# First layer's weights converted with an accumulating DMA, and one output chunk by seven products

## The chip, the cores and the metric

The kernel runs on 1 core of one Trainium2 chip. The metric is the device time of one execution in microseconds (us), the median of 3 runs. TensorE does the matrix products, VectorE (DVE) and ScalarE (ACT) the elementwise work, GpSimd (POOL) and SyncE (SP) issue transfers.

## The reference, cut to what matters

An attention over channels, then two feed-forward layers on 6016 tokens of 256 channels, all float32:

```
qn = q / (norm(q, axis=1) + 1e-6);  kn = k / (norm(k, axis=1) + 1e-6)
a  = softmax(kn^T @ qn / tau)            # 256 x 256
x  = (v @ a) as 6016 x 256
x  = gelu_sigmoid(x @ w_in) @ w_out      # layer 0: 256 -> 2048 -> 256
h  = x @ w2_in
out = (max(h, 0) + alpha * min(h, 0)) @ w2_out   # layer 1, same shapes
```

The weights are given as float64 and reach the kernel as pairs of 32-bit words.

## The kernel before

**Numbers in two parts.** Every operand of a product is a pair (hi, lo) of the fast 32-bit matmul type; a product is three matmuls, hi by hi, hi by lo and lo by hi (`PASSES`).

**Tiling.** The tokens are cut in 12 chunks, taken in 6 pairs, and each layer runs pair by pair. For each pair the hidden width is cut in 8 chunks j = 0 to 7 (`NQ`). For one j the kernel makes four hidden blocks ("units") and adds their share of the output (`Outs`, 8 steps of three matmuls; those of j run between the products of j + 1). The first pair of layer 0 goes by `direct`: each unit is two products, eight per j. All other pairs go by `quartet`: seven products per j (Strassen's scheme), on sums and differences of the operands, which `prepare` (tokens) and `combine_wi` (weights) build. In `quartet` the first product's result is copied from one PSUM bank to another by ScalarE, so that two later products add to it (`nc.scalar.copy(b, a)`, the copy of line 827, called "the fork copy" below).

**A unit in `direct`.** ScalarE takes the product out of PSUM (`act`, L761, writes `g`), rounds it to `ghi` (`high`, L775); VectorE writes the rest `glo` (`low`, L781), which the output step of the next j reads. Between `high` and `low`, `beside` puts background work for about 2.1 us on VectorE. ScalarE work that this asks for is kept in `put_off` and issued in one go at the start of the next `beside`, so after the next unit's `high`. Engines run in the order in which the program was written; a waiting instruction holds all behind it on its engine. Unit (j, u) below is the u-th of chunk j.

**Converting a weight piece.** During the first pair the background work is the conversion of layer 0's weights. A piece (class `Convert`) is 128 x 512 numbers of two words each: inner pieces ia0 to ia7 are one j's columns of `w_in`, outer pieces ob0 to ob7 one j's rows of `w_out`; from the fifth on, two neighbours are done as one piece of 1024. SP loads the raw words (2 `raw` buffers); ScalarE makes `p` from the high word (L130); VectorE does six steps: `shift` (L133), `signed` (L137, writes `top`), `power` (L147), `rest` (L150, puts the low word's share in `p`), `less` (L166), `low` (L169, writes the lo part). Between `signed` and `less` ScalarE rounds `top` to the hi part (`copy`, L143). A load goes out when the `rest` of the piece that had its buffer is done.

**What waits for a piece.** `emit_w(j)` (j up to 3) and `emit_pair(4)`, `emit_pair(6)` multiply ia pieces by the softmax's transpose on TensorE (L483, L628), and ScalarE (`keep_hi`, L491) and VectorE (`keep_lo`, L495) bring the result to `WI`, the inner weights that the units use. They stand after unit (j - 1, 1). The outer pieces feed the output steps of their j directly (`WO`).

Of the kernel before, what the change touches and what calls it, by code (L numbers as in the profile page):

```python
# [34 lines left out]
TAIL = 12  # L35
ON_VECTOR = (4, 5, 6, 8)
# [20 lines left out]
def attention_then_two_ffns(ctx: ExitStack, tc: tile.TileContext, q, k, vT, tau, w1i, w1o, w2i, w2o, alpha, outT):  # L57
# [45 lines left out]
    class Convert:  # L103
# [4 lines left out]
        most = 2 * PIECE  # L108
        pool = None

        def __init__(self, src, pair, done=None):
            self.src, self.pair, self.done = src, pair, done
            self.made = False
            self.a = src.shape[1]
            self.n = self.a * src.shape[2]
# [7 lines left out]
        def load(self):  # L123
            self.raw = self.tile("raw", U32, RAWS, 2)
            nc.sync.dma_start(self.raw.rearrange("p (a n) w -> p a (n w)", a=self.a), u32(self.src))

        def scale(self):

            self.p = self.tile("p", F32, 2)
# [5 lines left out]
        def signed(self):  # L135
            self.top = self.tile("top", F32, 1)
            nc.vector.scalar_tensor_tensor(u32(self.top), self.raw[:, :, 1], 0x80000000, u32(self.p),  # L137
                                           ALU.bitwise_and, ALU.bitwise_or)
            self.hi, self.lo = self.pair()
            put_off.append(self.copy)  # L140

        def copy(self):
            nc.scalar.copy(self.hi, self.like(self.top))  # L143
# [30 lines left out]
    class Converter:  # L174


        STEPS = (("shift", 0.45), ("signed", 0.7), ("power", 0.45), ("rest", 0.7), ("less", 0.7), ("low", 0.7))

        def __init__(self):
            self.todo, self.loaded, self.ready, self.open, self.at = [], [], [], None, 0  # L180

# [3 lines left out]
        def load(self):  # L185

            while self.todo and len(self.loaded) + len(self.ready) + self.held < RAWS:
# [4 lines left out]
        def scale(self):  # L192
            if self.loaded and not self.ready:
# [3 lines left out]

        def cost(self):
            return self.time(self.open or (self.ready + self.loaded + self.todo)[0])

        def time(self, piece):
            t = self.STEPS[self.at][1]
            return 2 * t - 0.15 if piece.n > PIECE else t

        def waits(self):

            if not self.open:
# [5 lines left out]
        def needs(self):  # L213
            return [self.ready[0].scale] if self.at == 0 else [self.open.copy] if self.at == 4 else []

        def step(self):

            if self.waits():
                scalar_work()
            if not self.open:  # L220
                self.open = self.ready.pop(0)
                self.held = 1
            do, t = self.STEPS[self.at][0], self.time(self.open)
            getattr(self.open, do)()
            self.at += 1
            if do == "rest":
                self.held = 0
                self.scale()
                if self.ahead:
                    self.load()  # L230
            if self.at == len(self.STEPS):
# [11 lines left out]
        def left(self):  # L243
            return self.todo + self.loaded + self.ready + [x for x in (self.open,) if x]
# [10 lines left out]
    with tc.manual_schedule():  # L255
# [15 lines left out]
        def inner(j, n=1):  # L271
# [8 lines left out]
            return Convert(w1i.rearrange("p (a n) -> p a n", a=2)[:, :, j * C:(j + n) * C], pair)  # L280

        def outer(j, n=1):
            def pair():
                return tuple(WO[:, j:j + n, h].rearrange("p q a b -> p q (a b)") if n > 1 else flat(WO[:, j, h]) for h in range(2))
            return Convert(w1o[:, j * PIECE:(j + n) * PIECE].rearrange("p (a n) -> p a n", a=1), pair)

        ia, ob_ = {}, {}
        for made, piece, spans in ((ia, inner, ((0, 1), (1, 1), (2, 1), (3, 1), (4, 2), (6, 2))),
                                   (ob_, outer, ((0, 1), (1, 1), (2, 1), (3, 1), (4, 2), (6, 2)))):
# [3 lines left out]
        conv.todo = [ia[1], ob_[0], ia[2], ob_[1], ia[3], ob_[2], ia[4], ob_[3], ob_[4], ia[6], ob_[6]]  # L293
# [19 lines left out]
        def operand(pool=None):  # L313
# [3 lines left out]
            slot[0] += 1  # L317
            return xin[i > 3].tile([P, 2, T], F32R, tag=f"x{i}", name="x")
# [225 lines left out]
        def prepare(l, p):  # L544
# [4 lines left out]
            ops = operands[l, p] = {}  # L549
# [40 lines left out]
            ]  # L590
            return early, late
# [191 lines left out]
        def direct(j, outs, mid_way):  # L783

            ops = operands[0, 0]
            units = []
            for i, (f, c) in enumerate((f, c) for f in range(2) for c in range(2)):
# [12 lines left out]
                beside(FIRST, convert=True)  # L800
# [4 lines left out]
        def quartet(l, p, j, outs, carry):  # L805
# [3 lines left out]
            late = steps_late if j == 0 else []  # L809

# [3 lines left out]
            def copy(ps):  # L814
                s = sp.tile([P, T], F32, tag="s", name="s", bufs=3)
# [285 lines left out]
```

## Time and profile before

| | |
|---|---|
| median of 3 runs | 1034.37 us (1034.36 to 1034.7) |
| the profiled execution | 1034.38 us |
| its span, first to last instruction | 1032.6 us |
| TensorE matmul busy | 1027.4 us |
| VectorE busy | 765.3 us |
| ScalarE busy | 752.8 us |
| GpSimd busy | 31.3 us |
| granted TensorE clock | 1.000 over the span |

How to read it: 1.8 us of the execution lie outside the span. The matmuls of the first pair begin at about 50 us and those of the second pair at about 142 us, all times from the span's start. A matmul row in the timeline gives the time at which it began and how long it took; the next one begins before it ends, so whether TensorE lost time is read from the distances between beginnings. An idle time in square brackets names what ended it.

### The profile page before, as it was taken

Reading aid. Unit: us, or ns where it says so; the run is one execution under the profiler, and the core shown is the slowest. Engines: PE = TensorE matmul, PEld = TensorE weight load, DVE = VectorE, ACT = ScalarE, POOL = GpSimd, SP = SyncE. Lnnn points to the kernel's source line nnn. Section 1 sums busy time; section 2 is a strip of 40 time slices with the busy share of each in tenths; the row PEclk is TensorE's granted clock in tenths of the full one; section 3 lists DMA queues with packets and bytes.
Section 4 is the critical chain, followed back from the end, with each engine's and each line's share of the span. In section 5 each row is a group of like instructions: output and inputs, shape, how many; then the busy total and the mean of one; then the engine's idle time right before and its main releaser. Section 6 shows DMA issues by size and latency. Waiting matters only on the chain.

```text
span 1032.6 us, 12486 instructions
## 1 busy us (share of the span) xinstructions
PE 1027.4 (99%) x4640; PEld 866.8 (84%) x4640; DVE 765.3 (74%) x1230; ACT 752.8 (73%) x1255; POOL 31.3 (3%) x42
## 2 busy tenths in 40 slices
PE   9999999999999999999999999999999999999998
PEld 8888888888888888888998888888888888888997
DVE  4889967878778787445637777787877787877766
ACT  6777767778777777666767777777777777867776
POOL 4400000000000000000100000000000000000000
PEclk9999999999999999999999999999999999999999
DMA  9635102125224323003543001001001000000101
GB/s 361 240 106 180 42 23 95 42 77 179 77 82 158 101 93 133 1 1 126 200 169 113 1 21 62 1 21 62 1 21 62 1 18 25 35 0 1 42 1 36
DMA packets 30461, 77.62 MB, mean 75 GB/s; under 512 B 3008, under 2 KB 7616, under 8 KB 30144
## 3 DMA queue, kind: packets, MB, share of 16 engines
q1 hardware_dynamic: 28096, 65.29, 18.2%
q0 software_dynamic: 2304, 11.54, 3.4%
q8 instruction: 36, 0.59, 0.2%
q14 instruction: 25, 0.20, 0.1%
HBM read 52.96 MB, written 23.86 MB: 74 GB/s over the span
## 4 chain that ended last, share of the span: by engine, by line
PE 99%; DMA 0%; SPq 0%; ACT 0%; issue 0%
PE ps_o L713 50%; PE ps_h L684 44%; PE gram L348 4%; PE pw L483 1%; PE pw L628 1%; DMA qk<-in_k 0%; SPq L368 0%; PE nrm L426 0%; ACT s L730 0%; PE bc L448 0%; PE pt L471 0%
## 5 line engine op out<-in xcount | busy, mean ns | idle before, releaser
L713 PE MATMUL ps_o<-ghi,wo 128*128 128x512 f32 (+1 forms) x1536 | 561.6, 385 | 0.0
L684 PE MATMUL ps_h<-x,wi 128*128 128x512 f32 (+1 forms) x2040 | 550.5, 385 | 0.0
L684 PEld LDWEIGHTS ps_h<-x,wi 128*128 128x128 f32 x2040 | 382.2, 188 | 72.4 <-DVE wi L495 0.4
L713 PEld LDWEIGHTS ps_o<-ghi,wo 128*128 128x128 f32 x1536 | 288.3, 188 | 53.5
L713 PE MATMUL ps_o<-glo,wo 128*128 128x512 f32 (+1 forms) x768 | 296.0, 385 | 0.0
L750 DVE TENSOR_TENSOR g<-ps_h,s 128x512 f32<-128x512 f32 (+1 forms) x177 | 120.0, 678 | 94.1 <-PE ps_h L684 60.4
L779 DVE SCALAR_TENSOR_TENSOR glo<-g,sign_sb,ghi 128x512 fp32r<-128x512 f32 (+1 forms) x192 | 141.4, 736 | 55.5 <-ACT ghi L773 51.1
L816 ACT COPY s<-ps_h 128x512 f32<-128x512 f32 (+1 forms) x177 | 102.2, 577 | 104.7 <-PE ps_h L684 100.4
L781 DVE TENSOR_TENSOR glo<-g,ghi 128x512 fp32r<-128x512 f32 (+1 forms) x192 | 126.4, 677 | 68.1 <-ACT ghi L775 67.9
L713 PEld LDWEIGHTS ps_o<-glo,wo 128*128 128x128 f32 x768 | 144.2, 188 | 27.3 <-DVE glo L779 0.3
L773 ACT ACTIVATE ghi<-g,sign_sb 128x512 fp32r<-128x512 f32 (+1 forms) x192 | 137.0, 714 | 16.1 <-DVE g L769 10.8
L775 ACT CAST ghi<-g 128x512 fp32r<-128x512 f32 (+1 forms) x192 | 113.3, 612 | 3.6
L761 ACT ACTIVATE g<-ps_h 128x512 f32<-128x512 f32 (+1 forms) x112 | 65.7, 587 | 44.6 <-PE ps_h L684 43.9
L765 ACT ACTIVATE g<-g,sign_sb 128x512 f32<-128x512 f32 (+1 forms) x97 | 69.5, 717 | 29.2 <-DVE g L750 28.6
L769 DVE SCALAR_TENSOR_TENSOR g<-g,slope_sb 128x512 f32<-128x512 f32 (+1 forms) x97 | 71.6, 738 | 16.8 <-ACT g L765 16.6
L769 DVE SCALAR_TENSOR_TENSOR g<-ps_h,slope_sb,g 128x512 f32<-128x512 f32 (+1 forms) x95 | 69.7, 733 | 0.0
L827 ACT COPY ps_h<-ps_h 128x512 f32<-128x512 f32 (+1 forms) x87 | 49.0, 563 | 28.2 <-PE ps_h L684 27.6
L765 ACT ACTIVATE g<-ps_h,sign_sb 128x512 f32<-128x512 f32 (+1 forms) x95 | 64.3, 676 | 2.2 <-ACT g L765 0.3
L761 ACT ACTIVATE g<-g 128x512 f32<-128x512 f32 (+1 forms) x80 | 49.8, 623 | 15.5 <-DVE g L750 15.3
L348 PE MATMUL gram<-qk 128*128 128x256 f32 x156 | 34.3, 380 | 0.3 <-DMA qk<-in_k 0.3
L348 PEld LDWEIGHTS gram<-qk 128*128 128x128 f32 x156 | 29.4, 190 | 4.6 <-issue 0.7
L563 DVE TENSOR_TENSOR x<-t,x 128x512 fp32r<-128x512 f32 (+1 forms) x44 | 29.0, 671 | 0.0
(115 smaller groups left out, 498.6 us busy)
## 6 DMA issues: line engine op xcount, KB each, us to landing
wi<-w2i POOLq DMA_DIRECT2D x8, 896.0 KB, 4.9
xraw<-in_vT SPq DMA_DIRECT2D x10, 512.0 KB, 6.1
x<-ob SPq DMA_DIRECT2D x20, 256.0 KB, 2.3
xraw<-x SPq DMA_DIRECT2D x10, 512.0 KB, 3.5
out_T<-ob SPq DMA_DIRECT2D x20, 256.0 KB, 2.1
qk<-in_q SPq DMA_DIRECT2D x9, 512.0 KB, 10.2
qk<-in_k SPq DMA_DIRECT2D x9, 512.0 KB, 10.3
raw<-in_w2i SPq DMA_DIRECT2D x8, 512.0 KB, 4.2
```

The lines of the kernel that those rows point to most:

```text
L348: nc.tensor.matmul(gram[m][:, :C], tiles[i][:, 1, r, m * P:(m + 1) * P], tiles[i][:, 0, r, :], start=(t == 0), stop=(t == R - 1))
L684: nc.tensor.matmul(ps[:, :n], WI[:, wq, a, blk], x[:, b, :n], start=(start and i == 0), stop=(stop and i == 2), skip_group_check=True)
L713: nc.tensor.matmul(acc_ps[c][d][:, :n], WO[:, j, a, f, d * P:(d + 1) * P], (hi, lo)[b][:, :n], start=(start and i == 0), stop=(stop and i ...
L750: nc.vector.tensor_tensor(self.src, ps[:, :self.n], s[:, :self.n], ALU.add)
L761: nc.scalar.activation(self.g, self.src, AF.Gelu_apprx_sigmoid)
L765: nc.scalar.activation(self.g, self.src, AF.Copy, scale=sign_sb[:, self.f])
L769: nc.vector.scalar_tensor_tensor(self.g, self.src, slope_sb[:, self.f], self.g, ALU.mult, ALU.max)
L773: nc.scalar.activation(self.hi, self.g, AF.Copy, scale=sign_sb[:, self.f])
L775: nc.scalar.copy(self.hi, self.g)
L779: nc.vector.scalar_tensor_tensor(self.lo, self.g, sign_sb[:, self.f], f32(self.hi), ALU.mult, ALU.subtract)
L781: nc.vector.tensor_tensor(self.lo, self.g, f32(self.hi), ALU.subtract)
L816: nc.scalar.copy(s[:, :n], ps[:, :n])
```

## The change

**Accumulating DMA.** Inner pieces from ia3 on and outer pieces from ob2 on are `added`: eleven pieces. VectorE does `shift`, `signed`, `power` and `rest`; then GpSimd's queue issues a DMA from SBUF to SBUF that adds `top` to `p` (`sent`). When it has landed, ScalarE rounds the sum to the hi part (`copy`, now from `p`), and VectorE writes the lo part as the sum less hi (`split`). While a piece's DMA flies, the steps of the next pieces run. `p` has 5 buffers, `top` 2, `raw` 3 instead of 2, 1 and 2; ScalarE makes `p` for two pieces ahead. All pieces are single now.

**Seven products.** Chunk j = 7 of the first pair goes by `quartet`. Its operands (`prepare(0, 0)` without the four blocks that are there already) and the weight sums of j = 7 are built in j = 4 to 6; the next pair's tokens are loaded in j = 6 instead of j = 3, and its operands and the weight sums of j = 0 are begun in j = 6. The weight sums of j = 1 move to the second pair, those of j = 7 away from it.

```diff
+STRASSEN = 7
         def load(self):
-            self.raw = self.tile("raw", U32, RAWS, 2)
+            self.raw = self.tile("raw", U32, Convert.raws, 2)
...
         def copy(self):
+            if self.added:
+                self.hi, self.lo = self.pair()
+                self.top = self.p
             nc.scalar.copy(self.hi, self.like(self.top))
...
+        def sent(self):
+            nc.gpsimd.dma_start(out=self.p, in_=self.top, accum_op=ALU.add)
+
+        def split(self):
+            nc.vector.tensor_tensor(self.lo, self.like(self.p), f32(self.hi), ALU.subtract)
+            self.made = True
...
+        ADDED = (("shift", 0.45), ("signed", 0.7), ("power", 0.45), ("rest", 0.7))
...
         def scale(self):
-            if self.loaded and not self.ready:
+            while self.loaded and len(self.ready) < 1 + (self.ahead and Convert.deep):
                 x = self.loaded.pop(0)
                 put_off.append(x.scale)
                 self.ready.append(x)
...
+        def landed(self):
+            return self.flying and self.flying[0].asked and self.flying[0].copy not in put_off
+
+        def ask(self):
+            if self.flying and not self.flying[0].asked:
+                self.flying[0].asked = True
+                put_off.append(self.flying[0].copy)
...
+        def settle(self):
+            self.flying.pop(0).split()
...
             if do == "rest":
                 self.held = 0
                 self.scale()
+                if self.open.added:
+                    self.ask()
                 if self.ahead:
                     self.load()
-            if self.at == len(self.STEPS):
+            if self.at == len(steps):
+                if self.open.added:
+                    self.open.sent()
+                    self.flying.append(self.open)
                 self.open, self.at = None, 0
...
-        conv.todo = [ia[1], ob_[0], ia[2], ob_[1], ia[3], ob_[2], ia[4], ob_[3], ob_[4], ia[6], ob_[6]]
+        conv.todo = [ia[1], ob_[0], ia[2], ob_[1], ia[3], ob_[2], ia[4], ia[5], ob_[3], ob_[4], ia[6], ia[7], ob_[5], ob_[6], ob_[7]]
...
+                if j == 4 and i == 0:
+                    sums0.extend(prepare(0, 0))
+                    bg.extend(sums0)
+                if j == 6 and i == 0:
+                    own_first[0] = False
+                    finish(sums0)
+                    for c in range(2):
+                        load_tokens(0, 2 + c)
+                if j == 6 and i == 2:
+                    pair1.extend(prepare(0, 1))
+                    bg.extend(pair1[0][:3])
+                    combining_of(0)
+                    bg.extend(pair1[0][3:])
+
+            if j < STRASSEN:
+                outs = direct(j, outs, mid_way)
+                continue
+            finish(combined[j])
...
+            outs = quartet(0, 0, j, outs, carry)
```

**Where instructions stand now.** VectorE in the first pair, from `keep_lo` of chunk 2 on, before (`p_622`, `top_626`, `wi_lo_564` are piece ia3, `glo_646` is unit (1, 2)):

```order
L495 SCALAR_TENSOR_TENSOR wi_436<-pw_650,rs_127,wi_436 128x256 x2
L150 SCALAR_TENSOR_TENSOR p_622<-raw_567,p_622 128x512
L166 TENSOR_TENSOR top_626<-top_626,wi_hi_563 128x512
L169 TENSOR_TENSOR wi_lo_564<-top_626,p_622 128x2x256
L781 TENSOR_TENSOR glo_646<-g_647,ghi_645 128x512
```

The lo part of ia3 is the third instruction after its `rest` is begun. The same place now (`p_584` and `wi_lo_569` are ia3, `p_627` is ob2, `p_698` is ia4, `glo_694` is unit (1, 2)):

```order
L556 SCALAR_TENSOR_TENSOR wi_438<-pw_655,rs_127,wi_438 128x256 x2
L158 SCALAR_TENSOR_TENSOR p_584<-raw_533,p_584 128x512
L137 TENSOR_SCALAR p_627<-p_627 128x512
L141 SCALAR_TENSOR_TENSOR top_677<-raw_572,p_627 128x512
L844 TENSOR_TENSOR glo_651<-g_652,ghi_650 128x512
L155 TENSOR_SCALAR p_627<-top_677 128x512
L158 SCALAR_TENSOR_TENSOR p_627<-raw_572,p_627 128x512
L137 TENSOR_SCALAR p_698<-p_698 128x512
L141 SCALAR_TENSOR_TENSOR top_706<-raw_603,p_698 128x512
L844 TENSOR_TENSOR glo_694<-g_695,ghi_693 128x512
L164 TENSOR_TENSOR wi_lo_569<-p_584,wi_hi_568 128x2x256
```

Nine instructions, among them all four steps of ob2 and two of ia4, now stand between `rest` and the lo part; `top_706` is the buffer that ia3's DMA reads from, so its instruction waits for that DMA.

ScalarE at the same place before, from `keep_hi` of chunk 2 to unit (1, 3) (`wi_hi_563` is the hi part of ia3):

```order
L491 ACTIVATE wi_436<-pw_650,rs_127 128x256 x2
L143 CAST wi_hi_563<-top_626 128x2x256
L761 ACTIVATE g_689<-ps_h_674 128x512
L775 CAST ghi_687<-g_689 128x512
L130 ACTIVATE p_692<-raw_598 128x512
L761 ACTIVATE g_714<-ps_h_699 128x512
L775 CAST ghi_712<-g_714 128x512
```

And now, to unit (2, 0) (`wi_hi_568` is the hi part of ia3, `raw_673` the raw words of ia5):

```order
L552 ACTIVATE wi_438<-pw_655,rs_127 128x256 x2
L824 ACTIVATE g_695<-ps_h_680 128x512
L838 CAST ghi_693<-g_695 128x512
L134 ACTIVATE p_698<-raw_603 128x512
L824 ACTIVATE g_724<-ps_h_709 128x512
L838 CAST ghi_722<-g_724 128x512
L134 ACTIVATE p_727<-raw_673 128x512
L151 CAST wi_hi_568<-p_584 128x2x256
L824 ACTIVATE g_752<-ps_h_737 128x512
```

The hi part of ia3 moved behind two more units and behind the scaling of ia5, whose raw words are loaded into the buffer that ia3's `rest` frees.

ScalarE at the first quartet before, from unit (7, 2) of the first pair to the first unit of the second:

```order
L761 ACTIVATE g_1323<-ps_h_1308 128x512
L775 CAST ghi_1321<-g_1323 128x512
L761 ACTIVATE g_1342<-ps_h_1327 128x512
L775 CAST ghi_1340<-g_1342 128x512
L827 COPY ps_h_1366<-ps_h_1365 128x512
L761 ACTIVATE g_1395<-ps_h_1366 128x512
```

And now, from unit (6, 3) to the first unit of the quartet of j = 7:

```order
L824 ACTIVATE g_1312<-ps_h_1297 128x512
L838 CAST ghi_1310<-g_1312 128x512
L620 CAST x_1281<-xraw_1237 128x512
L620 CAST x_1282<-xraw_1237 128x512
L620 CAST x_1283<-t_1284 128x512
L676 CAST wi_438<-s_1288 128x512
L620 CAST x_1293<-t_1294 128x512
L896 COPY ps_h_1333<-ps_h_1332 128x512
L824 ACTIVATE g_1352<-ps_h_1333 128x512
```

Five roundings for the second pair now stand between the last direct unit and the fork copy, where none stood.

## Rows read from the trace of the kernel before

**Rows 1.** The page: TensorE's busy time, and the chain that ended last.
```profile
PE 1027.4 (99%) x4640; PEld 866.8 (84%) x4640; DVE 765.3 (74%) x1230; ACT 752.8 (73%) x1255; POOL 31.3 (3%) x42
PE 99%; DMA 0%; SPq 0%; ACT 0%; issue 0%
```
**Rows 2.** Busy time by stretch: length, busy us (instructions) per engine, PEclk, DMA share, GB/s.
```profile
70.00:110.00 40.00, 40.00 (x184) 33.34 (x182) 38.87 (x54) 29.12 (x46) 0.00 (x0) 1.00 0.43 145
130.00:150.00 20.00, 20.00 (x90) 16.57 (x89) 11.55 (x27) 11.48 (x20) 0.00 (x0) 1.00 0.00 0
```
**Rows 3.** Timeline of TensorE: start us, us, engine, line, operation, tiles, shapes, count.
```profile
61.23 0.39 PE L713 MATMUL ps_o<-glo,wo 128*128 128x512 f32 x1
...
75.66 0.40 PE L483 MATMUL pw<-wi_lo,eT_hi 128*128 128x256 f32 x2
...
87.77 0.62 PE L628 MATMUL pw<-wi_hi,eT_hi 128*128 128x512 f32 x2
88.23 0.61 PE L628 MATMUL pw<-wi_lo,eT_hi 128*128 128x512 f32 x2
...
144.92 0.84 PE L684 MATMUL ps_h<-x,wi 128*128 128x512 f32 x3
```
**Rows 4.** Timeline of VectorE in the first pair.
```profile
58.13 0.48 DVE L495 SCALAR_TENSOR_TENSOR wi<-pw,rs,wi 128x256 fp32r<-128x256 f32 x1 [0.83 <-ACT wi L491]
...
60.32 0.69 DVE L781 TENSOR_TENSOR glo<-g,ghi 128x512 fp32r<-128x512 f32 x1
...
70.39 0.68 DVE L150 SCALAR_TENSOR_TENSOR p<-raw,p 128x512 f32<-128x512 uint32 x1
...
71.71 0.69 DVE L169 TENSOR_TENSOR wi_lo<-top,p 128x512 fp32r<-128x512 f32 x1
...
72.92 0.42 DVE L133 TENSOR_SCALAR p<-p 128x512 uint32<-128x512 uint32 x1
...
74.45 0.69 DVE L781 TENSOR_TENSOR glo<-g,ghi 128x512 fp32r<-128x512 f32 x1
75.05 0.68 DVE L150 SCALAR_TENSOR_TENSOR p<-raw,p 128x512 f32<-128x512 uint32 x1
...
81.15 0.48 DVE L495 SCALAR_TENSOR_TENSOR wi<-pw,rs,wi 128x256 fp32r<-128x256 f32 x1 [0.54 <-ACT wi L491]
```
**Rows 5.** Timeline of ScalarE, softmax and first pair.
```profile
41.79 0.37 ACT L429 COPY G<-gram 128x256 f32<-128x256 f32 x1 [1.74 <-PE gram L348]
...
59.77 0.67 ACT L130 ACTIVATE p<-raw 128x512 f32<-128x512 f32 x1
60.35 0.58 ACT L761 ACTIVATE g<-ps_h 128x512 f32<-128x512 f32 x1
...
76.47 1.15 ACT L130 ACTIVATE p<-raw 128x1024 f32<-128x1024 f32 x1 [0.59 <-DMA raw<-in_w1i]
```
**Rows 6.** DMA issues, some by the time of issue: queue, count, KB each, us to landing.
```profile
wo<-w2o POOLq DMA_DIRECT2D x1, 512.0 KB, 4.9
...
wo<-w2o POOLq DMA_DIRECT2D x1, 512.0 KB, 7.2
...
out_T<-ob SPq DMA_DIRECT2D x20, 256.0 KB, 2.1
...
raw<-in_w1i SPq DMA_DIRECT2D x1, 512.0 KB, 4.0
...
raw<-in_w1o SPq DMA_DIRECT2D x1, 512.0 KB, 3.5
```
**Rows 7.** Timeline of ScalarE at the first pair's end.
```profile
115.79 1.13 ACT L559 CAST x<-xraw 128x512 fp32r<-128x512 f32 x2
...
130.84 0.60 ACT L761 ACTIVATE g<-ps_h 128x512 f32<-128x512 f32 x1 [1.47 <-PE ps_h L684]
...
132.00 0.61 ACT L613 CAST wi<-s 128x512 fp32r<-128x512 f32 x1
...
141.72 0.60 ACT L761 ACTIVATE g<-ps_h 128x512 f32<-128x512 f32 x1 [1.47 <-PE ps_h L684]
```

More of the change, by code (lines that the diff above doesn't have):

```diff
@@ L103, in attention_then_two_ffns, with __init__ @@
     class Convert:
-        most = 2 * PIECE
+        most = PIECE
         pool = None
-        def __init__(self, src, pair, done=None):
-            self.src, self.pair, self.done = src, pair, done
+        deep = True
+        raws = 3
+        def __init__(self, src, pair, done=None, added=False):
+            self.src, self.pair, self.done, self.added = src, pair, done, added
+            self.asked = False
             self.made = False
@@ L196, in scale, with next, list @@
                 self.ready.append(x)
+        def next(self):
+            return self.open or (self.ready + self.loaded + self.todo + [None])[0]
+        def list(self, piece):
+            return self.ADDED if piece and piece.added else self.STEPS
         def cost(self):
-            return self.time(self.open or (self.ready + self.loaded + self.todo)[0])
+            return self.time(self.next())
         def time(self, piece):
-            t = self.STEPS[self.at][1]
-            return 2 * t - 0.15 if piece.n > PIECE else t
-        def waits(self):
+            if not piece:
+                return 0.7
+            if self.landed():
+                return 0.7
+            return self.list(piece)[self.at][1]
+        def landed(self):
[4 more added lines that the diff above has]
+                put_off.append(self.flying[0].copy)
+        def waits(self):
+            if not self.next():
+                self.ask()
+                return self.flying[0].copy in put_off
+            if self.landed():
+                return False
             if not self.open:
@@ L213, in needs @@
         def needs(self):
-            return [self.ready[0].scale] if self.at == 0 else [self.open.copy] if self.at == 4 else []
+            if not self.next():
+                return [self.flying[0].copy]
+            if self.landed():
+                return []
+            if self.at == 0:
+                return [self.ready[0].scale]
+            if self.open.added:
+                return [self.flying[0].copy] if self.at == 3 and len(self.flying) > 1 else []
+            return [self.open.copy] if self.at == 4 else []
+        def settle(self):
+            self.flying.pop(0).split()
         def step(self):
@@ L219, in step @@
                 scalar_work()
+            if not self.next() or self.landed():
+                self.settle()
+                return 0.7
             if not self.open:
@@ L284, in pair @@
                 return tuple(WO[:, j:j + n, h].rearrange("p q a b -> p q (a b)") if n > 1 else flat(WO[:, j, h]) for h in range(2))
[L285 removed]
+            return Convert(w1o[:, j * PIECE:(j + n) * PIECE].rearrange("p (a n) -> p a n", a=1), pair, added=j > 1)
         ia, ob_ = {}, {}
[L288 to L289 removed]
+        for made, piece, spans in ((ia, inner, [(j, 1) for j in range(NQ)]),
+                                   (ob_, outer, [(j, 1) for j in range(NQ)])):
             for j, n in spans:
@@ L590, in prepare @@
             ]
+            if (l, p) == (0, 0):
+                return [early[i] for i in (2, 3, 6, 7)] + [late[i] for i in (0, 1, 2, 4, 5)]
             return early, late
@@ L799, in direct @@
                 mid_way(i)
-                beside(FIRST, convert=True)
+                beside(FIRST, convert=not own_first[0])
                 u.low()
@@ L1028, in attention_then_two_ffns @@
                     first(rest + nxt_late)
-                if i == 0 and j + AHEAD < NQ:
-                    combined.append(combine_wi(j + AHEAD))
-                    first(combined[-1])
+                if i == 0:
+                    fresh = [n for n in ((1, 2) if j == 0 else (j + 2,)) if n < STRASSEN]
+                    combined.update({n: combine_wi(n) for n in fresh})
+                    first(sum((combined[n] for n in fresh), []))
                 outs = quartet(l, p, j, outs, carry)
```

80 lines of the change are left out of this document (50 added, 30 removed).

## The prediction, made before the change ran

> **What bounds the kernel now.** I read the page first: TensorE is busy 1027.4 of 1032.6 us, and the chain that ended last is TensorE for 99% [rows 1]. A busy TensorE in this page need not be one at its peak, so I then read the beginnings of its matmuls: from the first unit of the first pair to the end they follow each other at 0.22 to 0.23 us without a hole, 90 of them in 130 to 150 us [rows 2]. So the time is TensorE's own work, and two things alone can change it: fewer matmuls, or a matmul that has to wait. Third, the busy times by stretch: from 70 to 110 us VectorE is busy 38.9 of 40 us, while it idles 8.4 of 20 us from 130 to 150 [rows 2]. In the conversion VectorE works behind TensorE: it begins `rest` of ia3 at 70.39 and writes ia3's lo part at 71.71 to 72.40 [rows 4]; TensorE reads that at 75.66 [rows 3]. The reserve is 3.3 us. That is where I look.
>
> **What the change removes.** Chunk 7 of the first pair needs seven products instead of eight: 3 matmuls at 0.22 to 0.23 us, 0.7 us off TensorE's path. Eleven pieces lose `less` and `low` and gain `split`, about 0.69 each [rows 4]: at most 7.6 us of VectorE work (less where two pieces shared one instruction before). Against it stand nine instructions for the operands of pair 0, three kinds for the weight sums of chunk 7 and two additions in the quartet, some 10 us, of which 2.5 move back to the second pair. The 8.4 us that VectorE idles at the end of the pair hide that; if they were gone, TensorE would wait for the surplus. VectorE's total is thus no matter; its order is.
>
> **The start.** A third `raw` buffer sends ob0's load ahead of the tokens, so they land one load later on a full queue. ScalarE idles 1.74 us for the Gram matrix right behind its first use of them [rows 5], which covers it: nothing, and at most a few tenths if that cover is gone.
>
> **Scaling two ahead.** ScalarE's scaling of ob1, formerly behind ia2's copy, now stands before the first gelu: 0.58 us (59.77 to 60.35) [rows 5]. VectorE waits there for ScalarE (0.83 us at 58.13), and so slips by the same: `glo` of unit (0, 1) ends at 60.32 + 0.58 + 0.69 = 61.59, and TensorE wants it at 61.23 [rows 3, 4]. It loses 0.4 us, and VectorE is 0.58 us late from there.
>
> **The first piece by DMA, ia3.** `rest` ends at 70.39 + 0.68 + 0.58 = 71.65 [rows 4]. Now three things hang on it.
> (1) The accumulating DMA, 256 KB from SBUF added to SBUF, on GpSimd's queue. No row shows one. Bound from below: 2.1 us, 256 KB from SBUF on SP's queue. From above: 7.2 us, the slowest of 512 KB on GpSimd's queue; one with nothing queued before it took 4.9 [rows 6]. I take 4.9, since the queue is the same and both terms of the sum have to be read, 512 KB. It lands at 76.6.
> (2) The load of ia5 goes into the raw buffer that this `rest` frees: 4.0 us for 512 KB of `w_in` (3.5 for `w_out`) [rows 6], so 75.7. ScalarE has its scaling queued before ia3's copy (the second order block of ScalarE): done at 76.3. (ScalarE waited for such a load at this place before, until 76.47 [rows 5], but with ia3's copy long done.) Then ia3's copy waits for the DMA: 76.6 to 77.25. Behind it stand the gelus of units (2, 0) and on.
> (3) `signed` of ia4 overwrites the `top` that the DMA reads, so VectorE itself waits until 76.6. Then come `glo` of (1, 2) and the split, each 0.6 after the one before (74.45 to 75.05) [rows 4]: the split runs from 77.8 to 78.5.
> TensorE wanted that lo part at 75.66 [rows 3] and gets it at 78.55: **2.9 us lost by then**, the 0.4 from above among them. With 2.1 and 3.5 us for the transfers, ScalarE's copy ends at 76.4, the split at 77.15, and the loss is 1.5. With 7.2 us the DMA lands at 78.9, the split ends at 80.8, the loss is 5.2.
>
> **The next places.** Output 4's and 5's product wants hi of ia5 at 87.77 and lo at 88.23 [rows 3], now 2.9 later, 90.7 and 91.1. From the end of ia3's split VectorE has ten instructions of 0.35 to 0.7 us to ia5's `rest`, with two waits for ScalarE of about half a microsecond, as the 0.54 at 81.15 [rows 4]: it ends at 85.0. Plus 4.9 for the DMA, 0.6 for the copy, 0.7 for the split: lo at 91.3, so another 0.2 us. With the 7.2 us DMA, whose buffers then hold VectorE up again, it is 2.3. Later pieces have the delay as their reserve: ia7 is split near 110, and its product comes after 115.
>
> **The quartet of chunk 7.** The fork copy must be done when TensorE begins the third product, 144.92 - 141.72 = 3.2 us after the last direct unit's gelu begins [rows 3, 7] (the quartet at 142 us stands where j = 7's will). ScalarE now does gelu and rounding (130.84 to 132.00, 1.16 us), five roundings for the second pair (1.13 for two, so 2.8), and then the copy (0.6) [rows 7]: 4.6 us. TensorE waits 1.4 us. ScalarE's backlog is worked off in that wait, and the quartets behind it have their roundings between other copies, as before: nothing there.
>
> **Sum.** Against the profiled execution's 1034.38 us (0.01 from the median; 1.8 outside the span are unchanged): -0.7 + 2.9 + 0.2 + 1.4 = +3.8, so **1038.2 us**. The bounds of the transfers give -0.7 + 1.5 + 0 + 1.4 = +2.2 (1036.6) and -0.7 + 5.2 + 2.3 + 1.4 = +8.2 (1042.6).
>
> **The Trainium skill on the DMA.** VectorE's one-input step `shift` takes 0.42 us where two-input steps take 0.69 [rows 4], so it runs in a faster mode, in every piece, just when the DMAs are issued. The Trainium skill ("SBUF — State Buffer", section "SBUF: two separate sides") says that a DMA from GpSimd's queue can starve beside a VectorE operation in its two-port mode, since GpSimd then cannot write the descriptors. No run here shows it: the GpSimd transfers of rows 6 ran when no such step was about. By that rule the time is that of the third rival. The skill's "DMA: Bandwidth & Descriptors", section "Anatomy of one DMA — SWDGE (gpsimd) path", gives 2.0 us plus the bytes at 436 GB/s, an estimate of 2.6 us here; by it the load of ia5 decides alone and the sum is about +2.9.
>
> **Rivals.** First, nothing is late: 1034.4 - 0.7 = 1033.7, not slower. The place is ia3's lo part; this decides in its favour if the road from the end of `rest` to it takes under 4.0 us instead of 6.9, counted from 71.65 to 75.66. For it: VectorE gains up to 0.69 us per piece. Against it: the raw load (3.5) and the scaling (0.6) alone fill it, before copy and split. The fork copy would have to be in time as well. Second, the conversion keeps up and only the fork copy is late: 1033.7 + 1.4 = 1035.1, still no difference that can be told. Third, the accumulating DMA is much slower, 7.2 us and more, by reading its target besides or by starved descriptors: 1042.6 and up; against it, nothing but the 4.9 us of plain transfers. That the change doesn't do what it says (matmuls not saved) is excluded by its order of instructions.
>
> **How the numbers follow.** The forecast 0.58 (1036.6 to 1041), nothing late 0.13, only the fork copy 0.15, the slow DMA 0.12; 0.02 is left for a gain that I don't see. A measurement of this kernel tells some 0.2%, 2.1 us, from no change. A few hundredths of the forecast's own spread lie under that. So slower 0.64, same 0.34, faster 0.02. The range takes in both cases without a difference and the forecast with its upper half, 1033.5 to 1041.5; it leaves out about 0.12 above and a little below. The forecast's own range is 1036.6 to 1041.
>
> **What would show it.** In the changed kernel's trace: a wait of TensorE for ia3's lo part (the `pw` product near 76 us) of about 2 to 3 us, ended by VectorE's split; ScalarE idle before ia3's copy, ended by the DMA or by the load before it; DMAs on GpSimd's queue of 4 to 6 us; a wait of about 1.4 us of the third product of chunk 7. I am wrong if TensorE's beginnings near 76 us show no hole, if the DMAs land within 3 us, or if VectorE reaches ia3's `rest` well before 71 us.

## The result, and the profile after

The changed kernel takes 1042.32 us (median of 6, 1041.85 to 1042.64) against 1034.36 us, a ratio of 1.0076 with a 95% interval of 1.0063 to 1.0089: slower by 8.0 us, twice the 3.8 us that were forecast, and above the range. The profiled execution takes 1042.04 us, its span is 1040.2 us.

The page of the changed kernel, TensorE's busy time and the chain that ended last; it answers to [rows 1]:

```profile
PE 1029.6 (99%) x4637; PEld 867.9 (83%) x4637; DVE 767.0 (74%) x1254; ACT 757.8 (73%) x1270; POOL 41.0 (4%) x53
PE 92%; DVE 1%; ACT 1%; issue 1%; DMA 0%; DVEq 0%
```

Three matmuls fewer, and the chain that ends last now leaves TensorE several times. Busy times by stretch, columns as in [rows 2]:

```profile
70.00:110.00 40.00, 36.94 (x162) 30.50 (x161) 31.05 (x58) 24.92 (x44) 7.25 (x8) 0.96 0.69 164
130.00:150.00 20.00, 18.98 (x84) 15.40 (x83) 15.81 (x31) 13.29 (x24) 0.00 (x0) 1.00 0.05 19
```

From 70 to 110 us TensorE lacks 3.1 us and its granted clock is 0.96 in the mean. VectorE, busy for 38.9 us of that stretch before, now has 31.1: it waits too. Where TensorE lost time is seen in its beginnings; its timeline, to be held against [rows 3]:

```profile
49.86 0.51 PE L544 MATMUL pw<-wi_hi,eT_hi 128*128 128x256 f32 x2 [1.54 <-ACT eT_hi L537]
...
63.34 0.50 PE L776 MATMUL ps_o<-glo,wo 128*128 128x512 f32 x1 [0.16 <-DVE glo L844]
...
80.02 0.50 PE L544 MATMUL pw<-wi_hi,eT_hi 128*128 128x256 f32 x2 [2.23 <-ACT wi_hi L151]
81.36 0.80 PE L544 MATMUL pw<-wi_lo,eT_hi 128*128 128x256 f32 x2 [0.84 <-DVE wi_lo L164]
...
95.01 0.62 PE L691 MATMUL pw<-wi_hi,eT_hi 128*128 128x512 f32 x2
...
141.05 0.39 PE L776 MATMUL ps_o<-ghi,wo 128*128 128x512 f32 x1
142.46 0.96 PE L747 MATMUL ps_h<-x,wi 128*128 128x512 f32 x3 [1.02 <-ACT ps_h L896]
```

The `glo` product stands at 63.34 instead of 61.23, 2.1 us late. The lo part of chunk 3's product stands at 81.36 instead of 75.66: 3.6 us more. The pair's product stands at 95.01 instead of 87.77: 7.2 us late, so 1.5 more without any wait between. At the fork copy the beginnings are 1.4 us apart (141.05 to 142.46) instead of 0.2, so it adds 1.2 (the idle time in brackets, 1.02, is a little less), and three matmuls give 0.7 back: 7.2 + 1.2 - 0.7 = 7.7, against 7.6 between the spans.

The 1.5 us without a wait are clock. The stretches behind the hole, columns as in [rows 2], the third last being the granted clock:

```profile
80.00:81.00 1.00, 0.50 (x2) 0.30 (x2) 1.00 (x3) 0.97 (x2) 0.00 (x0) 1.00 0.95 205
81.00:82.00 1.00, 0.64 (x3) 0.64 (x4) 0.97 (x3) 0.25 (x2) 0.00 (x0) 0.61 0.31 57
82.00:83.00 1.00, 1.00 (x6) 1.00 (x6) 0.97 (x2) 0.97 (x2) 0.34 (x1) 0.50 0.03 4
83.00:84.00 1.00, 1.00 (x6) 0.99 (x5) 0.76 (x2) 0.97 (x3) 0.51 (x1) 0.50 0.81 127
84.00:85.00 1.00, 1.00 (x4) 0.77 (x3) 0.96 (x2) 0.73 (x2) 0.00 (x0) 0.69 0.75 205
85.00:86.00 1.00, 1.00 (x6) 0.81 (x5) 0.97 (x3) 0.00 (x0) 0.00 (x0) 1.00 1.03 286
```

After TensorE had stood still for 2.23 and 0.84 us, it ran at 1.2 instead of 2.4 GHz for some 3 us.

ScalarE and VectorE around the hole, from the same trace:

```profile
48.36 0.62 ACT L386 CAST x<-xraw 128x512 fp32r<-128x512 f32 x1 [1.48 <-PE gram L409]
...
78.02 0.66 ACT L134 ACTIVATE p<-raw 128x512 f32<-128x512 f32 x1 [2.91 <-DMA raw<-in_w1i]
79.35 0.62 ACT L151 CAST wi_hi<-p 128x512 fp32r<-128x512 f32 x1 [0.67 <-DMA p<-top]
...
141.84 0.57 ACT L896 COPY ps_h<-ps_h 128x512 f32<-128x512 f32 x1
```
```profile
72.69 0.68 DVE L158 SCALAR_TENSOR_TENSOR p<-raw,p 128x512 f32<-128x512 uint32 x1
...
79.41 0.69 DVE L141 SCALAR_TENSOR_TENSOR top<-raw,p 128x512 uint32<-128x512 uint32 x1 [2.98 <-issue]
80.02 0.69 DVE L844 TENSOR_TENSOR glo<-g,ghi 128x512 fp32r<-128x512 f32 x1
80.62 0.68 DVE L164 TENSOR_TENSOR wi_lo<-p,wi_hi 128x512 fp32r<-128x512 f32 x1
```

This is the forecast road: `rest`, DMA, copy behind the load and scaling of ia5, VectorE held at `top`, `glo`, split. (The profile names nothing that ended VectorE's 2.98 us; the DMA, issued at 73.70, lands 5.6 us later, at 79.30, just before.) It is 8.6 us from the beginning of `rest` to the end of the split. Eight instructions stand between the two, not the nine counted above the prediction. Issues in the windows of the first accumulating DMA and of the last one (KB each, us to landing):

```profile
raw<-in_w1i SPq DMA_DIRECT2D x1, 512.0 KB, 4.6
p<-top POOLq DMA_DIRECT2D x1, 256.0 KB, 5.6
...
p<-top POOLq DMA_DIRECT2D x1, 256.0 KB, 3.3
```

The eleven take 3.3 to 6.2 us, 4.8 in the median. The last three, with no raw load beside them, take 3.3.

What the forecast has no term for is the first row of ScalarE above: the third block's rounding waits 1.48 us for the Gram matmuls, and the softmax's hi part, which stands behind it on ScalarE, is late with it. Everything from 49.86 on is late by this.

### The profile page after: what moved, and what is told of

It reads as the page before. It is cut to its first block, busy times and chain, and to the rows that moved or that the text cites. A ratio compares the mean times of both kernels' runs of the same rounds, so it can differ in the third digit from the quotient of the medians.

```text
span 1040.2 us, 12564 instructions
## 1 busy us (share of the span) xinstructions
PE 1029.6 (99%) x4637; PEld 867.9 (83%) x4637; DVE 767.0 (74%) x1254; ACT 757.8 (73%) x1270; POOL 41.0 (4%) x53
## 4 chain that ended last, share of the span: by engine, by line
PE 92%; DVE 1%; ACT 1%; issue 1%; DMA 0%; DVEq 0%
PE ps_o L776 48%; PE ps_h L747 42%; PE pw L691 1%; PE pw L544 0%; DVE top L141 0%; DMA p<-top 0%; DVE glo L844 0%; ACT x L620 0%; DVE p L158 0%; ACT wi L552 0%; ACT g L824 0%; ACT L990 0%; ACT ghi L838 0%; DVE top L181 0%; DVE p L155 0%
## 5 line engine op out<-in xcount | busy, mean ns | idle before, releaser
L624 DVE TENSOR_TENSOR x<-t,x 128x512 fp32r<-128x512 f32 (+1 forms) x48 | 31.6, 672 | 0.0
```

## Experiments

Theory at the outset: the loss has four separate places, the start (a block's memory), the DMA's road to ia3, the clock behind the hole, and the fork copy. Rivals: the tokens' later loads, VectorE's added work, or a conversion that is late as a whole. All ratios are to runs of the kernel before on the same chip.

**The start.** The change also gives the first eight operand blocks a new order of places, in two lines that stand in no excerpt so far (the third line is as before):

```diff
+            if slot[0] <= 8:
+                i = (2, 1, 4, 0, 3, 5, 6, 7)[i]
             return xin[i > 3].tile([P, 2, T], F32R, tag=f"x{i}", name="x")
```

Places up to x3 lie in an early pool, those from x4 on in a pool that is opened over the memory of the attention's tiles. The third block, formerly at x2, now goes to x4. In this run the two places change pools: x4 lies in the early one, x3 in the one over the attention's tiles.

```diff
-            return xin[i > 3].tile([P, 2, T], F32R, tag=f"x{i}", name="x")
+            return xin[i == 3 or i > 4].tile([P, 2, T], F32R, tag=f"x{i}", name="x")
```

> Only the place of two operand blocks is swapped: the third block goes to the early pool, the fourth to the pool that lies over the attention's tiles. Theory A (the start's 1.7 us come from the third block's rounding waiting for the Gram matmuls, because its memory was theirs): the first matmul of the softmax product begins at 48.4 us again instead of 49.9, and the time falls by 1.7 us to 1040.6. Rival (the tokens land later behind the third raw buffer's load and hold the same rounding): the rounding then waits for a DMA instead, the product begins at 49.9 as before, and the time stays at 1042.3.

Measured: 1040.93 us (1040.14 to 1041.85), ratio 1.0060 (1.0045 to 1.0075). ScalarE's timeline, then TensorE's:

```profile
46.97 1.14 ACT L386 CAST x<-xraw 128x512 fp32r<-128x512 f32 x2
```
```profile
49.00 0.50 PE L544 MATMUL pw<-wi_hi,eT_hi 128*128 128x256 f32 x2
```

The two roundings follow each other, no wait is left, and the product begins right behind the last Gram matmul. (In this execution those matmuls themselves ended some 0.5 us later than before.) The time falls by 1.4 us (by 1.7 where each is held against the kernel before on its own chip); the place of the block is the cause, not the tokens' loads.

**The hole filled.** Matmuls whose result is overwritten stand ahead of chunk 3's product; seven more stand inside it. They reset the sums of that product, so that its output is not the reference's.

```diff
...
+            if j == 3:
+                for _ in range(10):
+                    nc.tensor.matmul(pw, WI[:, 0, 0, 0], blocks[0, 0][:, 0], start=True, stop=True, skip_group_check=True)
...
```

> The two holes of TensorE at the inner weights' product of chunk 3 are filled with matmuls whose result is overwritten (10 of 512 columns ahead of it, 7 of 256 columns between its hi and its lo part); nothing else changes. Theory A (TensorE's granted clock falls to half after it has stood still for some 3 us, and that costs 1.5 us more): PEclk stays 1.00 from 80 to 86 us, the matmuls there begin 0.22 us apart, and the time falls to 1040.8. Rival (the half clock has another cause, or the extra matmuls push the product back by as much): 1042.3 or a little more.

Measured: 1042.15 us (1041.74 to 1042.64), ratio 1.0070 (1.0053 to 1.0087). The stretch from 76 to 86 us, here and with the change as it is, then TensorE at the pair's product here:

```profile
76.00:86.00 10.00, 9.31 (x50) 7.92 (x49) 6.59 (x13) 5.19 (x9) 1.73 (x2) 1.00 0.81 205
```
```profile
76.00:86.00 10.00, 6.94 (x29) 5.65 (x29) 6.65 (x14) 5.20 (x9) 1.72 (x2) 0.83 0.81 203
```
```profile
95.10 0.73 PE L694 MATMUL pw<-wi_hi,eT_hi 128*128 128x512 f32 x2 [0.70 <-ACT wi_hi L151]
```

The clock stays at 1.00, as theory A has it (over the whole span 0.999 or 1.000 in all four executions, 0.998 in five of the change's six and 0.999 in one): without the hole it does not fall. But the time is not won. The seven matmuls inside the product came behind its wait and cost 0.8 us, and the pair's product, which waited for nothing, now waits 0.7 us for ia4's hi part. So the next pieces were just in time only because of the slow clock.

**The DMA one piece later.**

```diff
-            return Convert(w1i.rearrange("p (a n) -> p a n", a=2)[:, :, j * C:(j + n) * C], pair, added=j > 2)
+            return Convert(w1i.rearrange("p (a n) -> p a n", a=2)[:, :, j * C:(j + n) * C], pair, added=j > 3)
...
-            return Convert(w1o[:, j * PIECE:(j + n) * PIECE].rearrange("p (a n) -> p a n", a=1), pair, added=j > 1)
+            return Convert(w1o[:, j * PIECE:(j + n) * PIECE].rearrange("p (a n) -> p a n", a=1), pair, added=j > 2)
```

> Piece ia3 and piece ob2 are converted as in the kernel before; the accumulating DMA begins one piece later, with ia4 and ob3. Theory A (the wait for ia3 is that of the first piece by DMA alone, whose product comes 4 us after its rest): the 3.5 us wait at chunk 3's product and the 1.5 us of half clock behind it go, nothing takes their place, 1037.3. Rival 1 (VectorE, 1.4 us poorer, and the DMA make ia4 and ia5 late for the pair's product near 90 us instead): 1039 to 1041. Rival 2 (any first piece is late by as much): 1042.

Measured: 1042.74 us (1042.14 to 1042.96), ratio 1.0076 (1.0061 to 1.0091). TensorE's waits up to 170 us (total, times, longest):

```profile
PE pw L691 <- ACT wi_hi L151: 2.7, 1, 2.7
...
PE pw L691 <- DVE wi_lo L164: 0.6, 1, 0.6
```

Chunk 3 waits no more; the pair's product (L691) waits 2.7 and 0.6 us instead, with a clock of 0.83 from 90 to 100 us. Rival 2 holds for this piece: the first one by DMA is late here too. (It does not hold for every first piece; with six pieces, below, the first is in time.)

**The roundings behind the fork copy.** In the last direct unit `beside` issues one put-off operation instead of all.

```diff
-                beside(FIRST, convert=not own_first[0])
+                beside(FIRST, convert=not own_first[0], most=1 if (j, i) == (6, 3) else None)
```

> At the end of the last direct unit only one of the five put-off roundings for the second pair is issued ahead of the fork copy of chunk 7; the rest follow it. Theory A (the fork copy's wait of 1.0 us is those roundings): the third product of chunk 7 waits no more, 1041.3. Rival (the roundings are then missing where the next operands are made, and a later quartet waits instead): 1042.3 or more.

Measured: 1045.68 us (1044.86 to 1047.25), ratio 1.0107 (1.0092 to 1.0122). TensorE's timeline:

```profile
157.13 0.74 PE L747 MATMUL ps_h<-x,wi 128*128 128x512 f32 x2 [1.00 <-DVE x L624]
...
161.46 0.96 PE L747 MATMUL ps_h<-x,wi 128*128 128x512 f32 x3 [2.19 <-ACT s L885]
```

The wait at the fork is gone and 3.2 us of waits stand 15 us on. The roundings are needed where they are, or earlier; so earlier was tried (below).

**No DMA at all**, with the seven products kept: `added=False` in both of the lines shown two runs above.

> No piece is converted by DMA: all fifteen go through VectorE's six steps as in the kernel before; the third raw buffer, the scaling two ahead, the places of the blocks and the seven products stay. Theory A (the DMA's road alone makes the wait at chunk 3's product and, through it, the half clock): 3.5 and 1.5 us go, the start's 1.7 and the fork copy's 1.0 stay, 1037.3. Rival (VectorE, poorer by up to 7.6 us, is late elsewhere before the second pair): 1039 to 1042, with a wait for VectorE that is not there now.

Measured: 1046.07 us (1045.10 to 1047.14), ratio 1.0109 (1.0094 to 1.0125). TensorE's timeline:

```profile
136.60 0.73 PE L747 MATMUL ps_h<-x,wi 128*128 128x512 f32 x2 [1.17 <-ACT wi L676]
138.49 0.50 PE L747 MATMUL ps_h<-x,wi 128*128 128x512 f32 x1 [1.15 <-DVE wi L673]
...
153.68 1.65 PE L747 MATMUL ps_h<-x,wi 128*128 128x512 f32 x3 [3.54 <-ACT wi L676]
```

No hole near 76 or 88 us, but 5.9 us of waits for weight sums at chunk 7 and in the second pair, again with the clock down behind them (0.66 in the mean from 150 to 160 us). The rival holds: the seven products need the VectorE time that the DMA spares.

**The DMA without the addition**, which leaves the low word's share out of eleven pieces.

```diff
-            nc.gpsimd.dma_start(out=self.p, in_=self.top, accum_op=ALU.add)
+            nc.gpsimd.dma_start(out=self.p, in_=self.top)
```

> The same DMA without the addition: it copies top over p, so that the low word's share is left out of eleven pieces. Theory A (adding is what makes the transfer long, because the target is read besides): the eleven land in 2 to 3.5 us instead of 3.3 to 6.2, median 4.8, ia3's lo part is there 2 to 3 us earlier, and the time falls by 3 to 4 us. Rival (issue and the raw loads beside it make it long): landings at 4.8 in the median as now, and the time stays at 1042.3 within 0.5.

Measured, one execution: 1041.32 us. Issues in the windows of its first and its last DMA:

```profile
p<-top POOLq DMA_DIRECT2D x1, 256.0 KB, 4.8
...
p<-top POOLq DMA_DIRECT2D x1, 256.0 KB, 2.3
```

Piece by piece the addition costs 0.3 to 1.6 us of landing: 0.8 for the first (5.6 against 4.8) and 1.0 for the last (3.3 against 2.3), which has no raw load beside it. The eight transfers with a raw load beside them take 1.7 to 2.6 us longer than the three without (4.0 to 4.8 against 2.2 to 2.3), with the addition 1.0 to 2.9 us (4.3 to 6.2 against 3.3). That the load is the cause is read from which transfers run at the same time; no run takes it away. The rival is the nearer: the median is 4.5 against 4.8, and the time falls by 1.0 us where theory A has 3 to 4.

**Two roundings one unit earlier**, before the gelu of the last direct unit.

```diff
                 u.low()
+                if (j, i) == (6, 2):
+                    scalar_work(2)
```

> Two of the five roundings ahead of the fork copy are issued one unit earlier, before the last direct unit's gelu, where ScalarE idles for TensorE; no other instruction moves. Theory A (the fork copy's wait is ScalarE's queue of roundings, and ScalarE has room one unit earlier): the wait of 1.0 us at chunk 7's third product goes and nothing takes its place, 1041.3. Rival (the gelu of that unit then comes late, or the wait goes over to the next copies as it did when the roundings were put behind): 1042.3 or more.

Measured: 1041.10 us (1040.61 to 1042.37), ratio 1.0066 (1.0052 to 1.0080). The wait at the fork is gone and none took its place there. Two of the four executions, at a mean clock of 1.000, take 1040.61 and 1040.64; the two at 0.998 and 0.996 take 1041.56 and 1042.37. The profiled one, at 1.00 from 76 to 86 us in spite of the same hole (2.10 and 0.83 us), waits at the pair's product:

```profile
94.30 0.74 PE L691 MATMUL pw<-wi_hi,eT_hi 128*128 128x512 f32 x2 [0.82 <-ACT wi_hi L151]
```

So the clock does not fall after every such hole.

**Seven products and nothing else**: no DMA, two raw buffers and scaling one ahead, the blocks exchanged, the two roundings earlier.

```diff
-        deep = True
-        raws = 3
+        deep = False
+        raws = 2
...
```

> Seven products for chunk 7 without anything else that costs: no DMA, two raw buffers and scaling one ahead as in the kernel before, third block in the early pool, two roundings one unit earlier. Theory A (all the loss lies in the start, the DMA's road, the clock behind it, the scaling order and the fork copy, and VectorE's surplus fits in its idle time): 0.7 us are left as gain, 1033.7 against 1034.4. Rival (VectorE has some 10 us more to do before the second pair and idles 8.4): a wait for VectorE appears near the end of the first pair, 1035 to 1037.

Measured: 1041.90 us (1040.37 to 1043.66), ratio 1.0075 (1.0063 to 1.0088), with the waits of the run without DMA (4.7 us for ScalarE's weight sums, 1.1 for VectorE's). With the start, the scaling and the fork repaired, the seven products alone still cost more than they bring.

**The DMA alone**: eight products for chunk 7, blocks placed as in the kernel before; the operands for pair 0 and the weight sums of chunk 7 are left out with it.

```diff
-STRASSEN = 7
+STRASSEN = 8
...
-            if slot[0] <= 8:
+            if slot[0] <= 0:
...
```

> The DMA part alone: eleven pieces by accumulating DMA, third raw buffer, scaling two ahead; chunk 7 by eight products and the places of the blocks as in the kernel before. Theory A (the DMA's road costs by itself, whatever VectorE has to do): the wait at chunk 3's product is 3.5 us and the half clock behind it up to 1.5, with 0.6 from the tokens and 0.4 from the scaling, 1039 to 1040.5, and no wait at a fork copy. Rival (the loss comes from the operations that the seven products add for VectorE): within 1.5 us of the kernel before, 1034.4 to 1036.

Measured: 1041.46 us (1041.12 to 1042.98), ratio 1.0068 (1.0052 to 1.0085). TensorE's timeline:

```profile
78.57 0.50 PE L544 MATMUL pw<-wi_hi,eT_hi 128*128 128x256 f32 x2 [2.54 <-ACT wi_hi L151]
79.91 0.79 PE L544 MATMUL pw<-wi_lo,eT_hi 128*128 128x256 f32 x2 [0.84 <-DVE wi_lo L164]
```

The same hole and the same fall of the clock (0.83 from 76 to 86 us): theory A, though the time is 1 us above what it gave, 0.4 of that a wait for `glo` at 114.50. Its softmax product begins at 48.37, as in the kernel before, though the tokens land as late as in the change: their lateness costs nothing.

**All eleven by DMA, three repairs**: blocks exchanged and tokens loaded ahead of the later raw loads; scaling two ahead only from the second chunk on; two roundings earlier.

```diff
-            conv.held = 1
+            conv.held = 2
...
-            while self.loaded and len(self.ready) < 1 + (self.ahead and Convert.deep):
+            while self.loaded and len(self.ready) < 1 + (self.ahead and Convert.deep and self.late):
...
```

> All eleven pieces by DMA and seven products as in the change, with three repairs: third block in the early pool and the tokens' loads ahead of the second and third raw load; scaling two ahead only from the second chunk on; two roundings of the second pair one unit earlier. Theory A (the losses are separate): 1.7, 0.4 and 1.0 us go, the wait at chunk 3's product stays at 3.5 with its half clock, 1039.2. Rival (the pieces that follow are late by themselves, so that what is won is waited for at the pair's product near 90 us): 1040 to 1041.

Measured: 1038.97 us (1038.24 to 1039.64), ratio 1.0041 (1.0026 to 1.0056). What is left is the hole at chunk 3 (1.81 and 0.84 us) and a clock of 0.83 from 76 to 86 us. The repairs are worth 3.4 us, which bears out theory A's 3.1; a little of it is the hole, where chunk 3's lo part is 2.9 us late (78.55 against 75.66) instead of the 3.5 that theory A left there.

**The DMA only for pieces that are wanted late**, with the three repairs: first seven (ia6, ia7, ob3 to ob7: `added=j > 5` for inner, `added=j > 2` for outer pieces), then eight, with ob2 (`added=j > 1`).

> The three repairs, and the DMA only for the seven pieces that are wanted late (ia6, ia7, ob3 to ob7); ia3, ia4, ia5 and ob2 by VectorE's six steps. Theory A (the first pieces want the short road, the last ones spare VectorE what the seven products add): no wait at chunk 3's product or the pair's near 90 us, no half clock, seven times 0.69 us spared, so that of the 5.8 us that the kernel without DMA waits for the weight sums at most 1 is left, 1033.7 to 1035. Rival (VectorE is late for the weight sums of chunk 7 all the same): 1036 to 1040, with the half clock behind it.

> As the run with seven pieces by DMA, but ob2 by DMA too (eight pieces). Theory A (ob2 is read only by the output steps of the chunk after, and VectorE is spared 0.7 us more): 0 to 0.7 us under that run, 1033.7 to 1034.5. Rival (ob2's landing and split fall behind the first of these output steps, and TensorE waits there): 1 to 2 us over it.

Measured: seven 1035.55 us (1034.94 to 1036.46), ratio 1.0010 (1.0001 to 1.0019); eight 1044.48 us (1043.20 to 1044.83), ratio 1.0092 (1.0077 to 1.0107). TensorE's timeline with seven, then its waits with eight:

```profile
97.47 0.50 PE L777 MATMUL ps_o<-ghi,wo 128*128 128x512 f32 x1 [0.58 <-ACT wo L151]
...
98.81 0.50 PE L777 MATMUL ps_o<-ghi,wo 128*128 128x512 f32 x1 [0.60 <-DVE wo L164]
```
```profile
PE ps_o L777 <- ACT wo L151: 6.3, 1, 6.3
PE ps_o L777 <- DVE wo L164: 0.9, 1, 0.9
```

With seven, the loss at chunk 3, at the pair and at the weight sums is gone; the first piece by DMA, ob3, is late by 1.2 us. With eight, ob2 is late by 7, far more than either expectation has: in the code a piece's copy is asked for when the `rest` of the next `added` piece is done, and between ob2 and ob3 stand two plain pieces. The trace agrees: ob2's DMA, issued at 75.95, had landed 5.3 us later, at 81.3, but ScalarE's copy of it runs at 88.60, behind a scaling that waits until 88.02 for its raw load.

**Six and five pieces**: ob3 plain too (`added=j > 3` for outer pieces), then ob4 as well (`added=j > 4`).

> The three repairs, and the DMA for six pieces only: ia6, ia7 and ob4 to ob7; ob3 now by VectorE's six steps too. Theory A (the waits found so far are the whole loss): ob3's two waits of 0.6 us go, none takes their place, and what is left is the 0.7 us of three matmuls, 1033.7 to 1034.0 against 1034.4. Rival 1 (the first piece by DMA is late whichever it is): ob4's output step waits by 1 us or more, 1035 and up. Rival 2 (VectorE, poorer by 0.7 us, is late for the weight sums of chunk 7): a wait there, 1035 and up.

> As the run with six pieces, but five: ia6, ia7 and ob5 to ob7. Theory A (VectorE's idle time still holds the surplus): 1033.7 to 1034.2. Rival (each piece more on VectorE takes 0.7 us from the weight sums of chunk 7): a wait of up to 1 us there, 1034.5 to 1036 with a lower clock behind it.

Measured: six 1034.29 us (1033.95 to 1034.82) against 1034.31, ratio 1.0000 (0.9991 to 1.0009); five 1035.13 us (1034.56 to 1035.52), ratio 1.0007 (0.9998 to 1.0016). TensorE's waits with six, then with five:

```profile
PE ps_h L748 <- ACT ps_h L899: 0.3, 1, 0.3
PE pw L692 <- DVE wi_lo L164: 0.2, 1, 0.2
```
```profile
PE ps_h L748 <- ACT ps_h L899: 1.2, 1, 1.2
```

ScalarE's timeline with five, shortly before the fork copy, and then VectorE's at the `rest` of the last piece, with six and with five:

```profile
130.77 0.62 ACT L151 CAST wo<-p 128x512 fp32r<-128x512 f32 x1 [0.91 <-DMA p<-top]
```
```profile
115.99 0.69 DVE L158 SCALAR_TENSOR_TENSOR p<-raw,p 128x512 f32<-128x512 uint32 x1
```
```profile
126.43 0.69 DVE L158 SCALAR_TENSOR_TENSOR p<-raw,p 128x512 f32<-128x512 uint32 x1
```

Six pieces cost nothing any more, so the waits found are the loss. But the 0.7 us of three matmuls are not seen either: with six, both waits together stretch the distances of TensorE's beginnings by some 1.0 us. Five are one too few: the last piece's DMA now lands late, ScalarE waits 0.91 us for it, and the roundings and the fork copy behind it are late by as much. The DMA is late because VectorE, with one piece more to do itself, is 0.6 us behind and just misses its turn: in the code (`own_first`) the operands of pair 0 and the weight sums of chunk 7 go ahead of the conversion from unit (5, 1) on, and the last piece's `rest`, which with six begins at 115.99, ahead of them, comes behind them with five, at 126.43. The DMA is issued at 127.48 instead of 117.28. No kernel tried beats the one before by more than can be measured.

## Why the prediction was wrong

The direction and the main mechanism were right, the sum was half of what came. Three terms of it failed: the start and the clock, which it put at nothing, and the road of the first piece, which it made too short. By its own steps:

- **Three matmuls fewer**, -0.7: they show as a drop of the count by 3. Right.
- **The start**, nothing: it cost 1.4 us at the first softmax product and 1.7 us a few products on. This is the first step that failed. The prediction weighed the third raw buffer and the later tokens, and there it was right (the run of the DMA alone). It left out the new order of the blocks' places, which puts the third block into memory that the attention's tiles still hold; ScalarE's row at 48.36 shows the wait and the first run its removal.
- **Scaling two ahead**, 0.4: `glo` of unit (0, 1) lost 2.1 - 1.7 = 0.4. Right.
- **The first piece by DMA**, 2.5 on top of that: 3.6. The order of the road was right in every link, its lengths were too short: the DMA 5.6 instead of 4.9, the load of ia5 4.6 instead of 4.0, and they ran beside each other. This term was mis-sized by 1.1. Of the bounds the upper one, 7.2, was never reached.
- **The clock**: no term at all. The hole of some 3 us that the prediction itself forecast was followed by 3 us at half clock and cost 1.5 us more. This is the second step that failed. It could be seen in no row of before, where TensorE never stood still for that long in the first pair.
- **The next places**, 0.2: no wait, but because the slow clock gave the pieces 1.5 us; where the clock held (the filled hole, the earlier roundings) the pair's product waits 0.7 and 0.8 us. The term was real and too small, and it hides behind the clock's.
- **The fork copy**, 1.4: 1.2, by the five roundings as told.

1.7 for the start, 1.1 for the road, 1.5 for the clock, less 0.2 for the fork and 0.2 for the next places, are 3.9 of the 4.2 us that were missing; the rest is within the spread of runs.

**VectorE's total is no matter**, the prediction said, since its idle time at the pair's end hides the surplus. With the DMA that held. It holds only with it: without, 5.9 us of waits appear. Six spared pieces are enough; with five a wait of 1.2 us stands at the fork copy.

**The rivals.** That nothing is late, and that only the fork copy is, both fall. The slow DMA comes within 0.3 us of the time, but not by its mechanism: no landing is above 6.2 us. Of starved descriptors there is a small sign at most. GpSimd's rows for two issues of the changed kernel, then VectorE's step during the first of them:

```profile
98.00 1.02 POOL L161 DMA_DIRECT2D p<-top  x1 [5.38 <-DVE p L137]
102.64 0.85 POOL L161 DMA_DIRECT2D p<-top  x1 [3.63 <-DVE p L137]
```
```profile
98.50 0.43 DVE L155 TENSOR_SCALAR p<-top 128x512 uint32<-128x512 uint32 x1
```

The issue at 98.00, the only one of the eleven during which a whole one-input step of VectorE runs, took 1.02 us. The very first took 1.03, the other nine 0.85 to 0.88. With eight and with six pieces such a step falls into the first issue, which then takes 1.28; with five it does so too, and the issue takes 1.03. So it is a matter of some 0.2 us, and the landing at 98.00, 4.7 us, is not longer than its neighbour's, 4.8. The Trainium skill ("SBUF — State Buffer", section "SBUF: two separate sides") says that a DMA from GpSimd's queue can starve beside a VectorE operation in its two-port mode. The rows here neither rule this out nor make it a cause of the time.

The estimate of 2.6 us from the Trainium skill ("DMA: Bandwidth & Descriptors", section "Anatomy of one DMA — SWDGE (gpsimd) path") is near the 2.3 us of the plain transfer alone; with the addition it is 3.3, and beside a raw load 4.3 to 6.2.

What stays open: why the clock falls after one such hole and not after another. The length alone does not decide: after 1.81 and 0.84 us (three repairs) it fell, after 2.10 and 0.83 us (roundings earlier) it did not.

## What to carry to other kernels

Moving work from a busy engine to a DMA lengthens the road of each single piece, so give the DMA the pieces that are wanted late, and leave the first ones, whose consumer stands right behind, on the short road. When a change renames or reorders buffers, ask of every new place whose memory it was and when that is free: the first instruction that writes there waits for it too. Price a hole in TensorE above its own length, and when one wait is taken away, look what was late behind it: here part of what was won at chunk 3 was waited for again at the next piece.

## What the runs showed of the hardware

- An SBUF to SBUF transfer of 256 KB on GpSimd's queue landed in 2.2 to 2.3 us alone and in 4.0 to 4.8 us beside a raw load of 512 KB on SP's queue; with addition 3.3 and 4.3 to 6.2. GpSimd spent 0.54 to 0.70 us on the issue of a plain one, 0.85 to 1.03 on one with addition (1.28 in two runs, on the first issue).
- TensorE's granted clock went from 1.00 to 0.50 after holes of 2.2 and 0.8 us close together, and was back at 1.00 in the stretch from 85 us, some 3 us later. In the profiled execution with the blocks exchanged it was 0.66 in the mean from 76 to 86 us, lower than the 0.83 of the change, after a hole no longer (2.22 and 0.55 us); the pair's product then began at 94.92, only 0.1 us earlier than in the change, though chunk 3's lo part had begun 1.2 us earlier.
